# One operation of a search made one-input, and output weights split into their high and low parts once

## The chip, the cores and the metric

The kernel runs on one core of a Trainium2 chip. The metric is device time in microseconds (us), the median of several runs. TensorE (PE) multiplies matrices, PEld is its weight load; VectorE (DVE), ScalarE (ACT) and GpSimd (POOL) work on tiles; SyncE (SP) queues most transfers, POOL some of them.

## The reference

Three layers in a row, all float32: a linear attention with a norm, a mixture of eight experts in which every expert takes exactly 576 of 4608 tokens, and a layer that all tokens share.

```python
def _attn_ref(q, k, v, g_norm):
    kv = np.einsum('bhsd,bhse->bhde', k, v)
    out = np.einsum('bhsd,bhde->bhse', q, kv)
    rms = np.sqrt(np.mean(out * out, axis=-1, keepdims=True) + 1e-06)
    return (out / rms * g_norm).astype(np.float32)
...
def _moe_ref(x, w_gate, w1, w2):        # N=4608, D=512, E=8, F=1024
    cap = N // E
    logits = x @ w_gate
    order = np.argsort(-logits.flatten())
    # the highest logits first: a token goes to the expert of its highest logit that still has a place
    for e in range(E):
        out[assigned == e] = np.maximum(x[assigned == e] @ w1[e], 0.0) @ w2[e]
...
def _moe2_ref(x, w1, w2, w3, w_out):    # 512 -> 768 -> 512, weights shared by all tokens
    h = np.maximum(np.maximum(x @ w1, x @ w2), x @ w3)
    return (h @ w_out).astype(np.float32)
```

(The two lines on the assignment stand for a loop over the sorted logits.)

## The kernel before, in words

**Products.** Every large product is made of three matmuls on two float32r parts of each operand, `hi` (the value cast) and `lo` (value less `hi`): `mm3` (L823 to L825). One group is 12 such matmuls, [128x128] by [128x288].

**Stages.** Attention first; its rows go to the DRAM tile `xd`. Then one stage per expert, p = 0 to 7: gather the expert's 576 rows, w1 with relu (8 weight tiles), w2 (8 tiles), the shared layer's three products (18 tiles that stay in SBUF as `W3`), and the output product with the shared output weights `wo` (6 tiles). The tiles of w1, w2 and `wo` are streamed: `w_load` has SP fetch a [128x512] float32 tile into one of 3 buffers `raw`, and `w_split` makes `hi` (ACT, L349) and `lo` (POOL, L350, a subtraction with two inputs) in one of 6 buffers `ring`. So the six `wo` tiles are fetched and split again in each of the eight stages. `advance(n)` keeps splits three tiles ahead of PE.

**Routing beside it.** While stage p multiplies, the generator `phase(p + 1)` finds the next expert's tokens. `tick()` lets it go one piece further after each group of 12 matmuls, so its instructions stand between those of the stage in every engine's queue, in the order of the program. For p + 1 = 1 to 6 it runs `search` twice, with 11 and 5 steps. A step tests three thresholds: two counts on ACT (L490) and one on DVE (L492), `ce` (L496, DVE), a count over partitions on PE (L499), then on DVE `ex` (L503), `an` (L505), the step's sum `tot` (L507) and the next thresholds `T` (L511), for which L490 and L492 of the next step wait. A step spans two groups.

```python
nc.vector.scalar_tensor_tensor(ex[:, 0, 0:3], an, step, z, op0=OP.mult, op1=OP.add,
                               accum_out=tot)                      # L507, z is zeros
nc.vector.tensor_scalar(Tn, nx, T[:, 0:1], tot, op0=OP.add, op1=OP.add)   # L511
```

**The decoder.** The shared weights arrive as 64-bit words. `decoder` turns 24 tiles (18 of `W3`, 6 of `wo`, which stand first in `ORDER`, every second one) into float32 in the background, from the end of attention until the middle of stage 0: `dec_a` (ACT, L367 and L368, writes `dh` and `dr`), `dec_b` (DVE L376 and L378, POOL L379), `dec_c` one piece later, `dec_d` one more. A `W3` tile gets its `hi` in `dec_c` (ACT, L385) and its `lo` in `dec_d` (DVE, L393). A `wo` tile is stored in `dec_c` from POOL's queue into the DRAM tile `wod` (L387) and has nothing to do in `dec_d`.

Of the kernel before, what the change touches and what calls it, by code (L numbers as in the profile page):

```python
# [9 lines left out]
F32 = mybir.dt.float32  # L10
F32R = mybir.dt.float32r
# [4 lines left out]
OP = mybir.AluOpType  # L16
# [6 lines left out]
DM = NH * D  # L23
E = 8
FF = 1024
F2 = 768
# [10 lines left out]
def body(ctx: ExitStack, tc: tile.TileContext, qx, kx, vx, g, wg, w1, w2, w123, wo, out):  # L37
    nc = tc.nc
    consts = ctx.enter_context(tc.tile_pool(name="consts", bufs=1))
    dram = ctx.enter_context(tc.tile_pool(name="dram", bufs=1, space=DRAM))  # L40
    ctx.enter_context(tc.manual_schedule())

    xd = dram.tile([N, DM], F32, name="xd")
    wod = dram.tile([F2, DM], F32, name="wod")

    L = consts.tile([128, E, NT], F32, name="L")
    OWN = consts.tile([128, NT], F32, name="OWN")
# [18 lines left out]
    rt = ctx.enter_context(tc.tile_pool(name="rt", bufs=1))  # L66
# [93 lines left out]
    for s in range(2):  # L160
        p = slice(64 * s, 64 * s + 64)
        nc.vector.tensor_scalar(GW[p, :, s * E:s * E + E], wgt[p], gcol[p], None, op0=OP.mult)
    BD = []
    for i in range(2):
        t = ac.tile([128, NH // 2, 144], F32, name=f"BD{i}")
# [109 lines left out]
            nc.sync.dma_start(xd[c * 128:c * 128 + 128], xs)  # L275

    def keys(best, sh):
        """order-preserving integers of float32: the upper 32 - sh bits, the lower sh"""
        bi = best.bitcast(I32)
        sg, yy, hi, lo = (rt.tile([128, NT], I32, name="k" + str(i)) for i in range(4))  # L280
        sf = rt.tile([128, NT], F32, name="kf")
        nc.vector.tensor_scalar(sg, bi, 31, None, op0=OP.arith_shift_right)
        nc.vector.tensor_tensor(yy, bi, sg, op=OP.bitwise_xor)
        nc.vector.tensor_scalar(hi, yy, sh, None, op0=OP.arith_shift_right)
        nc.vector.tensor_scalar(lo, yy, 2 ** sh - 1, None, op0=OP.bitwise_and)
        nc.vector.tensor_scalar(sf, sg, 2.0 ** (31 - sh), 2.0 ** (31 - sh), op0=OP.mult, op1=OP.add)
        return sf, hi, lo

    def pick(V, oh, best, m):
        """one-hot of the first best expert"""  # L290
        def bb(ap):
            return ap[:, None, :].to_broadcast([128, E, NT])
        dv = desc[:, :, None].to_broadcast([128, E, NT])
        sc = rt.tile([128, E, NT], F32, name="scE")
        nc.vector.tensor_reduce(best, V.rearrange("p e c -> p c e"), axis=AX, op=OP.max)
        yield
        nc.vector.tensor_tensor(sc, V, bb(best), op=OP.is_equal)
        nc.vector.tensor_mul(sc, sc, dv)
        yield
        nc.vector.tensor_reduce(m, sc.rearrange("p e c -> p c e"), axis=AX, op=OP.max)  # L300
        nc.vector.tensor_tensor(oh, sc, bb(m), op=OP.is_equal)
        yield
# [45 lines left out]
    def split(raw, hi, lo, e):  # L348
        nc.scalar.copy(hi, raw)  # L349
        e.tensor_sub(lo, raw, hi)  # L350
# [3 lines left out]
    W3, XV = {}, {}  # L354
# [6 lines left out]
    def dec_a(i):  # L361
        while i not in W64:
            more64(1)
        w = W64.pop(i).rearrange("p (n t) -> p n t", t=2)
        h = early.tile([128, DM], F32, name="dh", bufs=3)
        r = early.tile([128, DM], I32, name="dr", bufs=5)
        nc.scalar.activation(h, w[:, :, 1].bitcast(F32), AF.Copy, scale=2.0 ** -112)  # L367
        nc.scalar.activation(r, w[:, :, 0].bitcast(U32), AF.Copy, scale=2.0 ** -29)  # L368
        XV[i] = (h.bitcast(I32), r)
        if i >= 18:  # L370
            late64.append(i - 6)
# [9 lines left out]
    def dec_c(i):  # L381
        v = XV[i][1].bitcast(F32)
        if i < 18:
            W3[i] = w3p.tile([128, 2, 512], F32R, name="w3_%d" % i, tag="w3_%d" % i)
            nc.scalar.copy(W3[i][:, 0], v)  # L385
        else:
            nc.gpsimd.dma_start(wod[(i - 18) * 128:(i - 17) * 128], v)  # L387

    def dec_d(i, e):
        v = XV.pop(i)[1].bitcast(F32)  # L390
        ready.append(i)
        if i < 18:
            e.tensor_sub(W3[i][:, 1], v, W3[i][:, 0])  # L393

    ORDER = [18, 0, 19, 1, 20, 2, 21, 3, 22, 4, 23, 5] + list(range(6, 18))
    ready, late64 = [], ORDER[12:18]
# [3 lines left out]
            load64(late64.pop(0))  # L400

    def decoder():
        """float64 words to float32, rounded to nearest, and to hi and lo"""
        for n in range(28):
            if n >= 4:
                dec_d(ORDER[n - 4], nc.vector)
            if 0 <= n - 3 < 24:
                dec_c(ORDER[n - 3])
            if n < 24:
                dec_a(ORDER[n])  # L410
            if 0 <= n - 2 < 24:
                yield from dec_b(ORDER[n - 2])
            yield
# [7 lines left out]
    for bp in range(NP):  # L421
# [31 lines left out]
        if bp == NP - 1:  # L453
# [3 lines left out]
            early = es.enter_context(tc.tile_pool(name="early", bufs=1, side="right"))  # L457
# [17 lines left out]
    ONE, IDX, IDXW = {}, {}, {}  # L475
# [2 lines left out]
        return ap[:, :, None].to_broadcast([128, E, NT])  # L478

    def search(KT, i0, i1, REM2):  # L480
        """the highest integer that leaves an expert with more keys from it on than it has places"""
        T = SC[:, i0]
        z = rt.tile([128, 3], F32, name="z")
        nc.vector.memset(z, 0.0)
        for i in range(i0, i1):
            cnt = rt.tile([96, 3], F32, name="cnt", bufs=2)
            gs = rt.tile([128, 36, 36], BF, name="W1", bufs=2)[0:96].rearrange("p a b -> p (a b)")
            gs = gs[:, 0:1152].rearrange("p (j a) -> p j a", j=3)
            for j in range(2):
                nc.scalar.activation(gs[:, j], KT, AF.Sign, bias=T[0:96, 1 + j:2 + j], scale=-1.0,  # L490
                                     accum_out=cnt[:, j:j + 1])
            nc.vector.tensor_scalar(gs[:, 2], KT, T[0:96, 3:4], -192.0, op0=OP.is_ge, op1=OP.add,  # L492
                                    accum_out=cnt[:, 2:3])
            yield
            ce = rt.tile([96, 3, E], BF, name="ce")
            nc.vector.tensor_mul(ce, BM, cnt[:, :, None].to_broadcast([96, 3, E]))  # L496
            yield
            pc = rps.tile([128, 512], F32, name="rps")
            nc.tensor.matmul(pc[:, :3 * E], ones[0:96], ce.rearrange("p j e -> p (j e)"), start=True, stop=True)  # L499
            ex = rt.tile([128, 3, E], F32, name="ex")  # L500
            an = rt.tile([128, 3], F32, name="an")
            tot = rt.tile([128, 1], F32, name="tot")
            nc.vector.tensor_tensor(ex, pc[:, :3 * E].rearrange("p (j e) -> p j e", e=E),  # L503
                                    REM2[:, None, :].to_broadcast([128, 3, E]), op=OP.is_gt)
            nc.vector.tensor_reduce(an, ex, axis=AX, op=OP.max)  # L505
            step = float(4 ** (10 - i) if i < 11 else 4 ** (15 - i))
            nc.vector.scalar_tensor_tensor(ex[:, 0, 0:3], an, step, z, op0=OP.mult, op1=OP.add,  # L507
                                           accum_out=tot)
            Tn = rt.tile([128, 4], F32, name="T4", bufs=2)
            nx = SC[:, i + 1] if i + 1 < i1 else SC[:, 16]  # L510
            nc.vector.tensor_scalar(Tn, nx, T[:, 0:1], tot, op0=OP.add, op1=OP.add)  # L511
            T = Tn
        yield T[:, 0:1]
# [7 lines left out]
        return dx  # L521

    def top_search(g2):
        """the first phase's search: thresholds at once, counted on the tensor engine"""
        def narrow(pc, J, i, K):
            ex = rt.tile([E, 64], BF, name="ex8")
            nc.vector.tensor_scalar(ex[:, 0:J], pc[0:E, 0:J], float(CAPN), None, op0=OP.is_gt)
# [12 lines left out]
        for it in range(6):  # L540
            if it == 4:
                K = rt.tile([128, NT], F32, name="K2")
                t = rt.tile([128, NT], F32, name="best")
# [200 lines left out]
    first = phase(0)  # L744
# [7 lines left out]
    stream = []  # L752
# [4 lines left out]
    RAW, RING, ROW = {}, {}, {}  # L757
    st = {"load": 0, "split": 0}

    def w_load():  # L760
        n = st["load"]
        st["load"] += 1
        p, kind, i = stream[n]
        raw = wr.tile([128, 512], F32, name="raw", bufs=3)
        RAW[n] = raw
        if kind == "wo":
            nc.sync.dma_start(raw, wod[i * 128:i * 128 + 128])
        else:
            if p not in ROW:
                ROW[p] = nc.values_load(IDXW[p][0:1, 0:1], engines=(mybir.EngineType.SP,), min_val=0,  # L770
                                        max_val=(E - 1) * 1024,
                                        skip_runtime_bounds_check_because="one of the experts")
            nc.sync.dma_start(raw, (w1 if kind == "w1" else w2)[bass.ds(ROW[p] + i * 128, 128), :])

    def w_split():
        n = st["split"]
        st["split"] += 1
        t = wr.tile([128, 2, 512], F32R, name="ring", bufs=6)
        split(RAW.pop(n), t[:, 0], t[:, 1], nc.gpsimd)
        RING[n] = t  # L780

    def advance(n):
# [36 lines left out]
        nc.vector.tensor_sub(X[:, :, 1, cs], src, X[:, :, 0, cs])  # L819

    def mm3(ps, wt, ws, x, xs, first, last):
        """exact products of hi and lo parts"""
        nc.tensor.matmul(ps, wt[:, 0, ws], x[:, 0, xs], start=first, stop=False)  # L823
        nc.tensor.matmul(ps, wt[:, 1, ws], x[:, 0, xs], start=False, stop=False)  # L824
        nc.tensor.matmul(ps, wt[:, 0, ws], x[:, 1, xs], start=False, stop=last)  # L825
# [198 lines left out]
```

## Time and profile before

| | before |
|---|---|
| median of 3 runs | 1310.72 us (1310.59 to 1311.41) |
| span of the profiled execution | 1307.6 us |
| what lies around the span (median less span) | 3.1 us |
| PE busy | 1200.0 us, 92% |
| DVE, ACT, POOL busy | 703.5, 503.3, 508.4 us |

No separate time is given for the profiled execution; its span is the first instruction to the last, and the median lies 3.1 us above it. Matmuls overlap in PE's pipeline, so PE's busy time says less than the distance from one matmul's start to the next.

### The profile page before, as it was taken

The page shows a single profiled execution, that of the slowest core. Times are in us where ns is not written, and L with a number is a line of the kernel's source. Part 1 is how long each engine was busy: PE and PEld are TensorE (multiplying, and loading weights), DVE is VectorE, ACT ScalarE, POOL GpSimd, SP SyncE. Part 2 cuts the span into 40 slices and gives each one's busy share as a digit, 9 for nine tenths or more (in the row PEclk, how much of TensorE's full clock was granted, in tenths as well). Part 3 has the DMA queues.
Part 4 walks back from the last instruction along what each step waited for, and adds up shares of the span by engine and source line. Part 5 has one row for each costly group of instructions (what it writes and reads, how often), then busy time and mean ns, then how long its engine had stood idle before and what let it go on. Part 6 is the DMA issues. An engine that isn't in the chain of part 4 may idle for free.

```text
span 1307.6 us, 23349 instructions
## 1 busy us (share of the span) xinstructions
PE 1200.0 (92%) x8814; PEld 1132.2 (87%) x8814; DVE 703.5 (54%) x2074; ACT 503.3 (38%) x1232; POOL 508.4 (39%) x539
## 2 busy tenths in 40 slices
PE   7796248899999999999999999999999999999997
PEld 6685238788889989998989998999899899989995
DVE  2799867897477427751776257734773231122110
ACT  3354426654354135522553245324541332133120
POOL 0456444434632435224422453145324372245231
PEclk9899559999999999999999999999999999999999
DMA  6978435400420113102320232013201151023101
GB/s 227 373 280 314 184 97 198 146 4 2 140 81 31 42 49 122 49 2 80 106 65 1 66 113 67 16 41 106 82 25 42 58 168 33 1 72 106 33 1 41
DMA packets 52689, 119.76 MB, mean 92 GB/s; under 512 B 6880, under 2 KB 11488, under 8 KB 51040
## 3 DMA queue, kind: packets, MB, share of 16 engines
q1 hardware_dynamic: 45712, 96.75, 22.4%
q0 software_dynamic: 6560, 21.50, 4.9%
q8 instruction: 69, 1.13, 0.4%
q14 instruction: 44, 0.36, 0.1%
q10 hardware_dynamic: 304, 0.02, 0.0%
HBM read 97.80 MB, written 20.45 MB: 90 GB/s over the span
## 4 chain that ended last, share of the span: by engine, by line
PE 60%; DVE 8%; ACT 4%; issue 3%; POOL 1%; DMA 0%; POOLq 0%; ACTq 0%; DVEq 0%
PE mm L823 16%; PE mm L825 16%; PE mm L824 16%; DVE ex L507 4%; ACT W L490 3%; PE mm L970 3%; PE mm L972 3%; PE mm L971 3%; PE tp L812 1%; DVE T L511 1%; DVE an L505 1%; DVE X L923 1%; DVE ex L503 0%; PE rps L615 0%; PE rps L499 0%
## 5 line engine op out<-in xcount | busy, mean ns | idle before, releaser
L823 PE MATMUL mm<-X,w 128*128 128x288 f32 x1152 | 345.3, 300 | 0.0
L350 POOL TENSOR_TENSOR ring<-raw,ring 128x512 fp32r<-128x512 f32 x176 | 228.8, 1305 | 299.6 <-ACT ring L349 285.9
L824 PE MATMUL mm<-X,w 128*128 128x288 f32 x1152 | 341.0, 296 | 1.5 <-DVE w L393 1.5
L825 PE MATMUL mm<-X,w 128*128 128x288 f32 x1152 | 341.1, 296 | 0.0
L824 PEld LDWEIGHTS mm<-X,w 128*128 128x128 f32 x1152 | 216.7, 188 | 2.2 <-DVE w L393 2.2
L823 PEld LDWEIGHTS mm<-X,w 128*128 128x128 f32 x1152 | 217.0, 188 | 0.4
L825 PEld LDWEIGHTS mm<-X,w 128*128 128x128 f32 x1152 | 216.4, 188 | 0.5
L947 POOL TENSOR_TENSOR H<-t,H 128x288 fp32r<-128x288 f32 x96 | 79.0, 823 | 339.3 <-ACT H L946 339.1
L945 DVE TENSOR_TENSOR t<-mm,t 128x288 f32<-128x288 f32 x192 | 87.0, 453 | 173.9 <-PE mm L825 173.6
L823 PE MATMUL mm<-X,ring 128*128 128x288 f32 x512 | 156.0, 305 | 2.1 <-ACT X L818 1.1
L823 PE MATMUL mm<-H,ring 128*128 128x288 f32 x512 | 155.5, 304 | 0.0
L824 PE MATMUL mm<-X,ring 128*128 128x288 f32 x512 | 152.2, 297 | 1.3 <-POOL ring L350 1.3
L825 PE MATMUL mm<-X,ring 128*128 128x288 f32 x512 | 152.4, 298 | 0.0
L824 PE MATMUL mm<-H,ring 128*128 128x288 f32 x512 | 151.3, 295 | 0.0
L825 PE MATMUL mm<-H,ring 128*128 128x288 f32 x512 | 151.2, 295 | 0.0
L490 ACT ACTIVATE W<-KT,T 96x384 bf16<-96x384 f32 x168 | 102.1, 608 | 126.2 <-DVE T L511 126.2
L946 ACT CAST H<-t 128x288 fp32r<-128x288 f32 x96 | 41.4, 431 | 255.0 <-DVE t L945 254.9
L349 ACT CAST ring<-raw 128x512 fp32r<-128x512 f32 x176 | 106.6, 615 | 6.3 <-DMA raw<-w_dram 6.3
L823 PEld LDWEIGHTS mm<-X,ring 128*128 128x128 f32 x512 | 97.9, 191 | 3.2 <-ACT X L818 1.9
L824 PEld LDWEIGHTS mm<-X,ring 128*128 128x128 f32 x512 | 97.6, 191 | 1.5 <-POOL ring L350 1.5
L825 PEld LDWEIGHTS mm<-X,ring 128*128 128x128 f32 x512 | 97.2, 190 | 0.3 <-DVE X L819 0.2
L823 PEld LDWEIGHTS mm<-H,ring 128*128 128x128 f32 x512 | 96.8, 189 | 0.0
(247 smaller groups left out, 2120.5 us busy)
## 6 DMA issues: line engine op xcount, KB each, us to landing
raw<-w_dram SPq DMA_DIRECT2D x128, 256.0 KB, 2.6
raw<-wod SPq DMA_DIRECT2D x48, 256.0 KB, 2.6
xd<-xs SPq DMA_DIRECT2D x36, 256.0 KB, 5.2
w<-w_dram SPq DMA_DIRECT2D x18, 512.0 KB, 4.7
qta<-qx_dram SPq DMA_DIRECT2D x4, 1280.0 KB, 11.1
qtb<-qx_dram SPq DMA_DIRECT2D x4, 1024.0 KB, 9.6
kta<-kx_dram SPq DMA_DIRECT2D x3, 1280.0 KB, 19.8
vta<-vx_dram SPq DMA_DIRECT2D x3, 1280.0 KB, 15.3
```

The lines of the kernel that those rows point to most:

```text
L349: nc.scalar.copy(hi, raw)
L350: e.tensor_sub(lo, raw, hi)
L490: nc.scalar.activation(gs[:, j], KT, AF.Sign, bias=T[0:96, 1 + j:2 + j], scale=-1.0, accum_out=cnt[:, j:j + 1])
L507: nc.vector.scalar_tensor_tensor(ex[:, 0, 0:3], an, step, z, op0=OP.mult, op1=OP.add, accum_out=tot)
L823: nc.tensor.matmul(ps, wt[:, 0, ws], x[:, 0, xs], start=first, stop=False)
L824: nc.tensor.matmul(ps, wt[:, 1, ws], x[:, 0, xs], start=False, stop=False)
L825: nc.tensor.matmul(ps, wt[:, 0, ws], x[:, 1, xs], start=False, stop=last)
L945: nc.vector.tensor_tensor(t2, ps[:, :HS], (t1, t1, t2)[j], op=OP.max)
L946: nc.scalar.copy(m[:, 0, cs], t2)
L947: nc.gpsimd.tensor_sub(m[:, 1, cs], t2, m[:, 0, cs])
L970: nc.tensor.matmul(pss[c], l[:, 0, ls], w[:, 0, :], start=(fc == 0), stop=False)
L971: nc.tensor.matmul(pss[c], l[:, 0, ls], w[:, 1, :], start=False, stop=False)
```

## The change

It does two things. The sum of a search step becomes a `tensor_scalar` that reads one tensor and also writes its sum; the tile of zeros `z` and its memset go. And the output weights are split once: `dec_c` casts a `wo` tile's `hi` into the old `dh` buffer (ACT), `dec_d` makes `lo` in `dr` (DVE) and stores both from POOL's queue into `wod`, which gets a middle dimension of 2; `dh` gets a fourth buffer. In the stages a `wo` tile is then fetched by one transfer of 512 KB straight into its `ring` buffer, in `w_split`, with no `raw` buffer and no split.

```diff
-    wod = dram.tile([F2, DM], F32, name="wod")
+    wod = dram.tile([F2, 2, DM], F32, name="wod")
...
-        h = early.tile([128, DM], F32, name="dh", bufs=3)
+        h = early.tile([128, DM], F32, name="dh", bufs=4)
...
         else:
-            nc.gpsimd.dma_start(wod[(i - 18) * 128:(i - 17) * 128], v)
+            nc.scalar.copy(XV[i][0].bitcast(F32R), v)
 
     def dec_d(i, e):
-        v = XV.pop(i)[1].bitcast(F32)
+        h, r = XV.pop(i)
+        v = r.bitcast(F32)
         ready.append(i)
         if i < 18:
             e.tensor_sub(W3[i][:, 1], v, W3[i][:, 0])
+        else:
+            e.tensor_sub(r.bitcast(F32R), v, h.bitcast(F32))
+            for j, t in enumerate((h, r)):
+                nc.gpsimd.dma_start(wod[(i - 18) * 128:(i - 17) * 128, j], t.bitcast(F32))
...
-        z = rt.tile([128, 3], F32, name="z")
-        nc.vector.memset(z, 0.0)
...
-            nc.vector.scalar_tensor_tensor(ex[:, 0, 0:3], an, step, z, op0=OP.mult, op1=OP.add,
-                                           accum_out=tot)
+            nc.vector.tensor_scalar(ex[:, 0, 0:3], an, step, 0.0, op0=OP.mult, op1=OP.add, accum_out=tot)
...
         p, kind, i = stream[n]
+        if kind == "wo":
+            return
         raw = wr.tile([128, 512], F32, name="raw", bufs=3)
         RAW[n] = raw
-        if kind == "wo":
-            nc.sync.dma_start(raw, wod[i * 128:i * 128 + 128])
...
         t = wr.tile([128, 2, 512], F32R, name="ring", bufs=6)
-        split(RAW.pop(n), t[:, 0], t[:, 1], nc.gpsimd)
+        if stream[n][1] == "wo":
+            i = stream[n][2]
+            nc.sync.dma_start(t.bitcast(F32), wod[i * 128:i * 128 + 128])
+        else:
+            split(RAW.pop(n), t[:, 0], t[:, 1], nc.gpsimd)
         RING[n] = t
```

On POOL, in stage 0 while the decoder runs (`dr` and `dh` are the decoder's buffers, L350 is the `lo` of a streamed tile), the order before is:

```order
L379 TENSOR_TENSOR dr<-dh,dr 128x512
L350 TENSOR_TENSOR ring<-raw,ring 128x512 x2
L379 TENSOR_TENSOR dr<-dh,dr 128x512
L350 TENSOR_TENSOR ring<-raw,ring 128x512
L387 DMA wod<-dr 128x512
L350 TENSOR_TENSOR ring<-raw,ring 128x512
L379 TENSOR_TENSOR dr<-dh,dr 128x512
```

and of the change, at the same place:

```order
L379 TENSOR_TENSOR dr<-dh,dr 128x512
L350 TENSOR_TENSOR ring<-raw,ring 128x512 x2
L379 TENSOR_TENSOR dr<-dh,dr 128x512
L350 TENSOR_TENSOR ring<-raw,ring 128x512
L398 DMA wod<-dh 128x512
L398 DMA wod<-dr 128x512
L350 TENSOR_TENSOR ring<-raw,ring 128x512
L379 TENSOR_TENSOR dr<-dh,dr 128x512
```

One store has become two, of the tile that was decoded one before, and the second waits for DVE's subtraction.

On ACT, in stage 0 (L902, L907 in the changed file, is the relu of a group; L490, L493 there, counts for the search), the order before is:

```order
L349 CAST ring<-raw 128x512
L902 ACTIVATE H<-mm 128x288
L367 ACTIVATE dh<-w_5_1386 128x512
L368 ACTIVATE dr<-w_5_1386 128x512
L902 ACTIVATE H<-mm 128x288
```

and of the change:

```order
L349 CAST ring<-raw 128x512
L907 ACTIVATE H<-mm 128x288
L387 CAST dh<-dr 128x512
L367 ACTIVATE dh<-w_5_1386 128x512
L368 ACTIVATE dr<-w_5_1386 128x512
L907 ACTIVATE H<-mm 128x288
```

A cast stands ahead of `dec_a`, whose two buffers are now those from which an earlier `wo` tile was stored.

On SP, at the end of stage 1's fetches (`idxw` holds the row of the next expert's weights, L773 fetches them), before:

```order
L773 DMA raw<-w_dram 128x512
L767 DMA raw<-wod 128x512 x6
L770 TENSOR_LOAD idxw
L773 ISA
L773 DMA raw<-w_dram 128x512
```

and of the change:

```order
L774 DMA raw<-w_dram 128x512
L782 DMA ring<-wod 128x1024 x4
L771 TENSOR_LOAD idxw
L774 ISA
L774 DMA raw<-w_dram 128x512
L782 DMA ring<-wod 128x1024
L774 ISA
L774 DMA raw<-w_dram 128x512
L782 DMA ring<-wod 128x1024
```

Two of the six `wo` fetches now stand behind the next expert's first fetches, and all six go to `ring`.

## Rows read from the trace of the kernel before

**Rows 1.** The page: span, and busy time of PE and its weight load.

```profile
span 1307.6 us, 23349 instructions
...
PE 1200.0 (92%) x8814; PEld 1132.2 (87%) x8814; DVE 703.5 (54%) x2074; ACT 503.3 (38%) x1232; POOL 508.4 (39%) x539
```

**Rows 2.** Windows: stretch, length, busy us (instructions) by engine, granted clock, DMA share, GB/s.

```profile
370.00:402.00 32.00, 29.36 (x213) 27.52 (x213) 24.44 (x78) 17.54 (x50) 11.56 (x9) 1.00 0.22 67
```

**Rows 3.** Waits of PEld, from 370 to 402, 205 to 300, whole run: us, times, longest.

```profile
PEld L499 <- DVE ce L496: 4.5, 8, 0.7
...
PEld L499 <- DVE ce L496: 11.7, 11, 1.9
...
PEld L499 <- DVE ce L496: 35.4, 56, 1.9
```

**Rows 4.** Timeline of PE around two steps: start, us, instruction, idle before it.

```profile
373.00 0.29 PE L825 MATMUL mm<-H,ring 128*128 128x288 f32 x1
373.74 0.19 PE L499 MATMUL rps<-ce,ones 96*128 96x24 bf16 x1 [0.44 <-DVE ce L496]
...
388.39 0.29 PE L825 MATMUL mm<-H,ring 128*128 128x288 f32 x1
388.82 0.19 PE L499 MATMUL rps<-ce,ones 96*128 96x24 bf16 x1
```

**Rows 5.** Timeline of POOL, DVE and ACT, one search step from 370 to 375.

```profile
370.43 1.28 POOL L350 TENSOR_TENSOR ring<-raw,ring 128x512 fp32r<-128x512 f32 x1 [2.64 <-ACT ring L349]
370.67 1.06 DVE L507 SCALAR_TENSOR_TENSOR ex<-an,z 128x3 f32<-128x3 f32 x1
371.77 0.29 DVE L511 TENSOR_SCALAR T<-SC,T,tot 128x4 f32<-128x4 f32 x1
372.16 0.62 ACT L490 ACTIVATE W<-KT,T 96x384 bf16<-96x384 f32 x1 [1.50 <-DVE T L511]
373.66 0.61 ACT L349 CAST ring<-raw 128x512 fp32r<-128x512 f32 x1
374.35 1.29 POOL L350 TENSOR_TENSOR ring<-raw,ring 128x512 fp32r<-128x512 f32 x1 [2.63 <-ACT ring L349]
```

**Rows 6.** Timeline of DVE, a step of the second search.

```profile
407.59 0.16 DVE L507 SCALAR_TENSOR_TENSOR ex<-an,z 128x3 f32<-128x3 f32 x1
...
407.79 0.29 DVE L511 TENSOR_SCALAR T<-SC,tot 128x4 f32<-128x4 f32 x1
```

**Rows 7.** Timeline of POOL and DVE in stage 0, from 229 to 231.

```profile
229.07 1.29 POOL L350 TENSOR_TENSOR ring<-raw,ring 128x512 fp32r<-128x512 f32 x1 [2.64 <-ACT ring L349]
229.41 0.97 DVE L507 SCALAR_TENSOR_TENSOR ex<-an,z 128x3 f32<-128x3 f32 x1
230.32 1.28 POOL L379 TENSOR_TENSOR dr<-dh,dr 128x512 int32<-128x512 int32 x1
230.43 1.20 DVE L511 TENSOR_SCALAR T<-SC,T,tot 128x4 f32<-128x4 f32 x1
```

**Rows 8.** Timeline of POOL and DVE in stage 0, at 256.

```profile
256.34 1.28 POOL L379 TENSOR_TENSOR dr<-dh,dr 128x512 int32<-128x512 int32 x1
256.44 0.61 DVE L492 TENSOR_SCALAR_CACHE_REDUCE W<-KT,T 96x384 bf16<-96x384 f32 x1
```

**Rows 9.** Timeline of PE and DVE in the first expert's top search.

```profile
154.06 0.17 PE L530 MATMUL rps<-ex,ones 8*128 8x15 bf16 x1 [0.25 <-DVE ex L527]
...
157.69 0.68 DVE L393 TENSOR_TENSOR w<-dr,w 128x512 fp32r<-128x512 f32 x1
...
158.83 0.17 PE L530 MATMUL rps<-ex,ones 8*128 8x15 bf16 x1 [0.56 <-DVE ex L527]
```

**Rows 10.** The stores of L387 by their landing; POOL and ACT where two of them fall.

```profile
DMA to landing us min/median/max: 2.5/3.9/4.5
...
225.12 1.30 POOL L350 TENSOR_TENSOR ring<-raw,ring 128x512 fp32r<-128x512 f32 x1 [2.03 <-ACT ring L349]
...
233.74 0.68 ACT L367 ACTIVATE dh<-w 128x512 f32<-128x512 f32 x1
```

**Rows 11.** The page's DMA issues: count, KB each, median us to landing.

```profile
w<-w_dram SPq DMA_DIRECT2D x18, 512.0 KB, 4.7
```

More of the change, by code (lines that the diff above doesn't have):

```diff
@@ L763, in w_load @@
         p, kind, i = stream[n]
+        if kind == "wo":
+            return
         raw = wr.tile([128, 512], F32, name="raw", bufs=3)
         RAW[n] = raw
-        if kind == "wo":
-            nc.sync.dma_start(raw, wod[i * 128:i * 128 + 128])
[L768 to L773, printed above, removed]
+        if p not in ROW:
+            ROW[p] = nc.values_load(IDXW[p][0:1, 0:1], engines=(mybir.EngineType.SP,), min_val=0,
+                                    max_val=(E - 1) * 1024,
+                                    skip_runtime_bounds_check_because="one of the experts")
+        nc.sync.dma_start(raw, (w1 if kind == "w1" else w2)[bass.ds(ROW[p] + i * 128, 128), :])
     def w_split():
```

## The prediction

> **What bounds the kernel now.** I read the page first: PE is busy for 1200.0 of 1307.6 us, the next engine for 703.5 [rows 1]. So the time can only move where PE stands still, or where its work changes; the change leaves PE's work alone. The windows come next. From about 300 us on PE stands still in one kind of stretch only, the second half of stages 1 to 5, where the search runs beside the products: from 370 to 402 it is busy for 29.36 of 32.00 us at full granted clock [rows 2]. The waits of its weight load say for what: `ce` of the count at L499, 4.5 us in 8 waits there, 11.7 us in 11 in stage 0, 35.4 in the whole run [rows 3]. Five stages and stage 0 make 34.2 of these 35.4. Of a wait's length a little is hidden in the pipeline, so I count PE's loss from starts: one matmul follows another by 0.13 us, L499 starts 0.74 after the last one, so 0.61 is lost; two steps later in the pattern 0.30 [rows 4]. The eight gaps of that stage are 0.61, 0.60, 0.32, 0.59, 0.30, 0.61, 0.30, 0.61, together 3.9 us; five such stages hold 19.5, and stage 0 another 11.
>
> What makes `ce` late is one step's timeline. L507 needs 0.16 us [rows 6], but takes 1.06 when POOL subtracts at the same time: it started at 370.67, POOL's L350 had started at 370.43 and ended at 371.71, and L507 ended at 371.73 [rows 5]. A DVE operation with two inputs in SBUF is held until POOL's operation ends. Then come the read of the sum and L511, 0.29, so that `T` is there 0.35 after POOL, and ACT's next count (L490) starts at 372.16 [rows 5]. ACT waits for `T`, `ce` for ACT, PE for `ce`, and the next split is queued behind PE's next group: a loop whose longest link at each held step is POOL's subtraction.
>
> **The sum of a step.** L507 gets one tensor instead of two. Its work should stay at 0.16; the nearest row is L492, also a `tensor_scalar` that writes its sum, on 128 times as many elements a lane: 0.61 [rows 8]. That is a ceiling of 0.61 and a floor of nothing saved; I take 0.16, since three elements cost what the old form on three costs. Whether it is held is told by the same row: POOL's L379 ran from 256.34 to 257.62, L492 started at 256.44 and took its usual 0.61 [rows 8]. So the new L507 is not held, and is done with its read about 0.26 after it starts.
>
> But right behind it stands L511, a plain `tensor_scalar`, and stage 0 shows that this one is held too: it took 1.20 instead of 0.29 and ended at 231.63, when POOL's L379, begun at 230.32, ended at 231.60 [rows 7]. So the wait doesn't go away, it moves one instruction down. L511 will stand there while POOL subtracts and end 0.04 after it, instead of 0.35: what is saved at a held step is 0.31, the read and L511's own work, which now lie under POOL's. Two bounds: L511 not held at all (the whole gap goes), or the new L507 held after all (nothing).
>
> 0.31 off each gap of the stage makes 0.30, 0.29, 0.01, 0.28, 0, 0.30 for the first six, 1.18 together. The last two follow steps in which the splits are those of `wo`; these splits go (next part), so nothing is held there and both gaps close. The stage loses 3.92 less 1.18, that is 2.74; five stages 13.7 us.
>
> **Weights split once.** Per `wo` tile and stage this removes a cast on ACT, 0.61, and a subtraction on POOL, 1.29 [rows 5]: 48 of each, 29 us of ACT and 62 of POOL. By itself that is worth nothing, since PE is ahead of neither; what counts is three subtractions per stage that fall into the search, already counted in the two closed gaps. The price is a fetch of 512 KB instead of 256 KB. The nearest row of that size lands in 4.7 us [rows 11], at a DMA share of 0.22 in such a stretch [rows 2]. A `wo` tile's `ring` buffer is free from the products of w2 on, tens of us before PE comes to the output product, so a fetch of 4.7, or of twice that, is hidden by the 18 tiles of `W3` that PE works on between. On SP two of the six fetches now stand behind the next expert's row number and first w1 fetches; these wait for nothing that they did not wait for before, and the `wo` tile behind them is needed a whole product later. I cost this at nothing; without that cover each late tile would cost PE its landing.
>
> **The decoder.** Each of six `wo` tiles gains a cast on ACT (0.61, by L349), a subtraction on DVE (0.68, by L393) and a second store; 12 memsets of `z` go, on an idle DVE. In the top search of the first expert a DVE subtraction of this kind, L393, lengthened PE's wait from 0.25 to 0.56 [rows 9]; two of the new ones fall there: 0.7. Three of the casts fall in stage 0's search, where ACT's counts are in the chain: up to 0.61 each, I take 0.5, so 1.5. The other subtractions meet a DVE that waits for ACT: 0 to 1.2, I take 0.5. Together 2.7, from 0.7 to 4.
>
> Stage 0 also gains. In five steps there POOL runs L350 and L379, or two L350, back to back; today L507 is held by the first and L511 by the second, as at 229.41 and 230.43 [rows 7]. Now L511 alone has to get in, and it can after the first: L507 ended at 230.38 although L379 had begun at 230.32 [rows 7], so an operation that already waits goes ahead of the next one on POOL. That is 1.2 a step, as far as the gap behind it reaches: the gaps are 0.74, 1.31, 1.13, 1.30 and 1.80, so 0.74 + 1.2 + 1.13 + 1.2 + 1.2, about 5.5. Bounds: 0, if the second on POOL gets in first, and 11, all of stage 0's gaps. The Trainium skill, "SBUF — State Buffer", section "Who interferes with whom", says that DVE and GpSimd share one pair of ports as an exclusive lock, and that whoever issues first keeps it for the whole instruction. By issue order alone the waiting L511 has it before L379, which is what the row shows; by a reading in which POOL's queue holds on to it, 5.5 would be 0.
>
> **Sum.** 13.7 + 5.5 - 2.7 = 16.5 us less. The profiled span of 1307.6 becomes 1291.1, and with the 3.1 us by which the median lies above that span [rows 1], 1294.2.
>
> **The rivals.**
>
> *L511 escapes as well.* If it is held only where it is the second of two, all 19.5 us in five stages go, 6 or more in stage 0, less 2.7: 23 us, 1287.8. Against it: the L511 of rows 7 started while L379 was 0.11 us old and was held to its end; the new one meets L350 in the same way.
>
> *The new sum is held too*, so the change doesn't do what it says. Then only the two gaps behind the `wo` splits close, 0.91 in each of five stages, 4.5, less 2.7: about 1309, not to be told from before. Against it speaks L492 of rows 8, which differs in its shape and in an output of half the width.
>
> *Slower: ACT waits for the stores.* `dec_a` writes the buffers from which a `wo` tile was stored, one step earlier than before. The second of the two stores stands in POOL's queue behind an L350 such as that at 225.12 (done at 226.42) and DVE's subtraction; with up to 1.6 us for the latter it goes at 226.5 to 228. The stores of today land in 3.9, at most 4.5 [rows 10]: by 232.5 at the latest. The L367 that needs the buffer starts at 233.74 [rows 10], so the slack is 1.2 us or more. If stores land later than that, ACT stands at L367, behind it the relu that frees PSUM and the counts of the search, and PE waits. Three tiles are exposed. To eat 16.5 us each would have to be held for 5.5, that is landing after 239.2, some 11 us after issue, over twice the longest of today. At 14 us each tile waits 8.3, and the time is about 1319. The Trainium skill, "SBUF — State Buffer", box "The 'DVE blocks DMA' trap (SWDGE)", says that a store queued by GpSimd can't have its descriptors written while DVE holds the shared ports; by its two figures (620 ns alone, 3100 overlapped) an estimate is 2.5 us more a store, a wait of up to 1.3 us a tile, and 1298 in place of 1294. None of the six stores of today is that late [rows 10].
>
> *Half the gain.* The loop of a stage could settle on another pace: with the counts sooner, ACT's casts and counts meet in another order, and 0.15 instead of 0.31 is saved a step, or stage 0 gains nothing. That is 8 to 11 us: 1300 to 1303.
>
> **How the numbers follow.** A measurement of this kernel can tell about 0.2%, 2.6 us. Chances: L511 takes over the wait 0.62, L511 escapes 0.12, half the gain 0.13, sum still held 0.08, stores late 0.05. The time of the likeliest is 1294.2, its own range 1290 to 1299 (its bounds of 4 and 0.7 for the decoder, of 0 and 8 for stage 0). From 1287 to 1303 leaves out the two on the slow side, 0.13, and a little beyond escape. Faster 0.87, same 0.08, slower 0.05.
>
> **What the profile after would show.** L507 at 0.16 to 0.2 in nearly all its 96 instances, and L511 at up to 1.1 in held steps, ending when POOL's L350 ends. PEld's wait at L499 down from 35.4 to some 12 to 15. L349 and L350 at 128 instances instead of 176. In a stage of 1 to 5, eight gaps with 1.2 us in all. Two waits at L530 longer by 0.3. It would be wrong if L511 stays at 0.29 beside POOL (faster than I say), if L507 still reaches 1.06 (no change), if ACT's L367 waits for a DMA from `dh` or `dr`, or if PE waits for `ring` from a DMA in the output product.

## The result, and the profile after

The changed kernel takes 1288.87 us, median of 4 runs (1288.18 to 1290.69), against 1311.07 us for the kernel before beside it. The ratio is 0.9827, interval 0.9810 to 0.9844: 22.2 us less, where 16.5 less were forecast. The time lies in the stated range, near its lower end, and below the 1290 to 1299 given for the likeliest case.

The page of the profile after answers to [rows 1]: PE's work is the same, POOL and ACT have less.

```profile
span 1288.9 us, 23207 instructions
...
PE 1197.7 (93%) x8814; PEld 1134.3 (88%) x8814; DVE 675.3 (52%) x2068; ACT 481.8 (37%) x1190; POOL 450.3 (35%) x497
```

Next the waits of PEld after (us in total, times, longest). In the changed file `ce` is L499 and its count L502.

```profile
PEld L502 <- DVE ce L499: 11.9, 24, 1.3
```

35.4 us in 56 waits [rows 3] have become 11.9 in 24. Where they went is told by the two lines of the change, by form (ns min/median/max): L510 is the sum, L513 the next thresholds `T` (L507 and L511 before).

```profile
L510 DVE TENSOR_SCALAR_CACHE_REDUCE ex<-an x96: 155/156/158, 222.8 to 956.5; 128x3 f32<-128x3 f32 x96
...
L513 DVE TENSOR_SCALAR T<-SC,T,tot x84: 287/428/1353, 226.6 to 956.7; 128x4 f32<-128x4 f32 x84
...
L513 DVE TENSOR_SCALAR T<-SC,tot x12: 287/290/827, 223.0 to 943.5; 128x4 f32<-128x4 f32 x12
```

The sum is never held: 158 ns at most in 96 steps, where L507 took 1.06 us [rows 5]. `T` is held in its place. One step, from the timelines of POOL and DVE (start, us):

```profile
373.56 1.29 POOL L350 TENSOR_TENSOR ring<-raw,ring 128x512 fp32r<-128x512 f32 x1 [2.31 <-ACT ring L349]
...
373.80 0.16 DVE L510 TENSOR_SCALAR_CACHE_REDUCE ex<-an 128x3 f32<-128x3 f32 x1
373.88 0.08 DVE L510 DVE_READ_ACCUMULATOR ex<-an 128x1 f32 x1
374.00 0.87 DVE L513 TENSOR_SCALAR T<-SC,T,tot 128x4 f32<-128x4 f32 x1
```

POOL's subtraction ends at 374.85, L513 at 374.87: 0.02 behind it. Before, `T` stood 0.35 behind POOL [rows 5]. PE's side of two steps in that stage:

```profile
376.55 0.19 PE L502 MATMUL rps<-ce,ones 96*128 96x24 bf16 x1
379.87 0.19 PE L502 MATMUL rps<-ce,ones 96*128 96x24 bf16 x1
383.43 0.19 PE L502 MATMUL rps<-ce,ones 96*128 96x24 bf16 x1
```

The steps are 3.32 and 3.56 us apart; 3.32 is the step in which PE waits for nothing. Of nine gaps, 4.1 us with the first of 0.18, three are left: 0.28, 0.24 and 0.25.

**Where the time went.** Whole profiled spans hold a difference that isn't the change's: the first count of the top search, ahead of which the change touches almost nothing, starts at 143.00 after, at 139.55 before. It starts at 143.00 in the kernel with the sum alone too, which changes nothing ahead of it. So I measure from there, by the starts of PE: first count of the top search, first and 16th count of the search in stage 0, 96th count (stage 5), last matmul. For the changed kernel:

```profile
143.00 0.21 PE L532 MATMUL rps<-ex,ones 8*128 8x63 bf16 x1 [0.30 <-DVE ex L529]
...
222.13 0.19 PE L502 MATMUL rps<-ce,ones 96*128 96x24 bf16 x1
...
281.12 0.19 PE L502 MATMUL rps<-ce,ones 96*128 96x24 bf16 x1
...
955.83 0.19 PE L502 MATMUL rps<-ce,ones 96*128 96x24 bf16 x1
...
1278.59 0.40 PE L977 MATMUL mm<-ring,H 128*128 128x512 f32 x1
```

The distances of such rows, in us, for each kernel (the experiments are told below):

| | to the search | stage 0's search | to the 96th count | to the end | sum |
|---|---|---|---|---|---|
| before | 77.91 | 63.95 | 692.64 | 323.66 | 1158.16 |
| after | 79.13 | 58.99 | 674.71 | 322.76 | 1135.59 |
| sum alone | 77.84 | 61.59 | 676.83 | 323.66 | 1139.92 |
| wo alone | 80.71 | 63.28 | 688.38 | 323.67 | 1156.04 |
| places alone | 77.94 | 63.82 | 691.37 | 322.76 | 1155.89 |
| after, old places | 80.81 | 59.04 | 676.11 | 323.66 | 1139.62 |
| decoder's work alone | 79.49 | 64.15 | 693.15 | 323.66 | 1160.45 |
| after, `T` freed | 79.19 | 58.73 | 670.44 | 322.76 | 1131.12 |
| after, `T` and `ce` freed | 79.36 | 60.27 | 670.48 | 322.75 | 1132.86 |

After less before: +1.22, -4.96, -17.93 and -0.90, together -22.57, which agrees with the 22.2 of the medians. The -0.90, in the column "to the end", was a surprise: no search runs there, and nothing was forecast.

### The profile page after: what moved, and what is told of

It reads as the page before. It is cut to its first block, busy times and chain, and to the rows that moved or that the text cites. A ratio compares the mean times of both kernels' runs of the same rounds, so it can differ in the third digit from the quotient of the medians.

```text
span 1288.9 us, 23207 instructions
## 1 busy us (share of the span) xinstructions
PE 1197.7 (93%) x8814; PEld 1134.3 (88%) x8814; DVE 675.3 (52%) x2068; ACT 481.8 (37%) x1190; POOL 450.3 (35%) x497
## 4 chain that ended last, share of the span: by engine, by line
PE 64%; DVE 5%; ACT 3%; issue 3%; POOL 1%; POOLq 0%; ACTq 0%; DVEq 0%
PE mm L828 18%; PE mm L829 17%; PE mm L830 17%; PE mm L975 3%; PE mm L977 3%; PE mm L976 3%; ACT W L493 3%; DVE T L513 2%; PE tp L817 1%; DVE an L508 1%; DVE ex L510 0%; PE rps L617 0%; DVE ex L506 0%; DVE X L928 0%; DVE H L910 0%
## 5 line engine op out<-in xcount | busy, mean ns | idle before, releaser
L350 POOL TENSOR_TENSOR ring<-raw,ring 128x512 fp32r<-128x512 f32 x128 | 167.5, 1311 | 259.3 <-ACT ring L349 237.3
L493 ACT ACTIVATE W<-KT,T 96x384 bf16<-96x384 f32 x168 | 102.1, 609 | 107.0 <-DVE T L513 107.0
L828 PEld LDWEIGHTS mm<-H,ring 128*128 128x128 f32 x512 | 96.8, 189 | 0.0
L829 PEld LDWEIGHTS mm<-H,ring 128*128 128x128 f32 x512 | 96.4, 188 | 0.0
```

## The experiments

**What bounds each half of the change.** The main theory: the two-input sum was the held operation, and `T` now takes its place. The rival: the three splits that left each search freed it. The first two kernels make one half each.

The sum alone, with `z` kept so that no tile moves:

```diff
-            nc.vector.scalar_tensor_tensor(ex[:, 0, 0:3], an, step, z, op0=OP.mult, op1=OP.add,
-                                           accum_out=tot)
+            nc.vector.tensor_scalar(ex[:, 0, 0:3], an, step, 0.0, op0=OP.mult, op1=OP.add, accum_out=tot)
```

> The kernel before with the one-input step sum alone; z and its memset stay, so that no tile moves, and the wo tiles are split in every stage as before. By the theory of the prediction (the wait moves from the sum to the T operation, 0.3 us shorter a step, and in stage 0 one hold takes the place of two) it carries most of the gain: some 3.0 us in each of five stages and 5 in stage 0, 18 to 21 us less, 1290 to 1293. By the rival that it is the removal of the wo splits that frees the search, it gains under 8 us, above 1303. In the trace: the sum at 0.16 us in all 96 instances, the T operation at up to 1.2.

Measured: 1294.54 us against 1312.86, ratio 0.9861 (0.9843 to 0.9880), 18.3 us less. This half carries most of the gain, so the rival falls. Its waits of PEld, and its `T` operation by form (L510 in this file):

```profile
PEld L499 <- DVE ce L496: 15.7, 29, 2.3
```

```profile
L510 DVE TENSOR_SCALAR T<-SC,T,tot x84: 288/765/1326, 225.2 to 960.1; 128x4 f32<-128x4 f32 x84
```

Here the median step is a held one, 765 ns. By stretch (table): 2.4 us off in stage 0, where 5 were expected, and 15.8 in the five stages, where 15 were. In stage 0 the wait moved one operation further in two steps: `ce`, which has two inputs as well and takes 0.18 us alone, was held by POOL for 1.28 and 1.25, and PE's gaps there are 1.68 and 2.25 us. The second stands beside the split of a `wo` tile:

```profile
258.45 1.46 POOL L350 TENSOR_TENSOR ring<-raw,ring 128x512 fp32r<-128x512 f32 x1
...
258.69 1.25 DVE L496 TENSOR_TENSOR ce<-BM,cnt 96x24 bf16<-96x24 f32 x1
```

The output weights alone, the old sum and `z` put back into the changed kernel (the diff above, reversed):

> The changed kernel with the old two-input step sum and z put back: the output weights alone are split once. By the theory the two gaps behind the old wo splits close, 0.9 us in each of five stages, 4.5 in all, and the decoder costs 1 to 2.7: 1.8 to 3.5 us less, 1307.5 to 1309.5. By the rival that fewer splits free the search as a whole it gains 10 us or more. If the stores held up the decoder, it would be slower than before.

Measured: 1310.20 us against 1312.86, ratio 0.9976 (0.9965 to 0.9987), 2.7 us less by the medians and 3.2 by the ratio, as the theory had it. The old sum is held as ever where POOL still splits:

```profile
L512 DVE SCALAR_TENSOR_TENSOR ex<-an,z x96: 161/268/1082, 221.8 to 973.5; 128x3 f32<-128x3 f32 x96
```

The median fell from 0.9 us to 0.27, because the steps behind the `wo` splits are free; the longest is the same 1.08. The table has 4.3 us off in the five stages and 0.7 in stage 0, and 2.8 added ahead of the search.

**The gain where no search runs.** In the changed kernel the matmuls of the shared products follow one another faster. Two theories: less work on the other engines, or the place of the tiles, since without `z` all that is allocated behind it (X, H, `raw`, `ring`) lies 32 bytes lower. Two kernels, one that moves only the tiles, and one that changes everything but their place:

```diff
-    SC = consts.tile([128, 17, 4], F32, name="SC")
+    SC = consts.tile([128, 18, 4], F32, name="SC")
...
-        z = rt.tile([128, 3], F32, name="z")
-        nc.vector.memset(z, 0.0)
+        z = SC[:, 17, 0:3]
```

The second is the changed kernel with the two removed lines put back; nothing reads its `z`.

> The kernel before in which z is a row of the constant tile SC instead of a tile of its own: no instruction of the steps changes (only 12 memsets go), but X, H, raw and ring lie 32 bytes lower, as in the changed kernel. The trace after shows the matmuls of the shared products 0.8 ns closer to each other than before, in stages 6 and 7 as well, where no search runs: some 0.33 us in each of eight stages. If the place of the tiles makes this, 2.0 to 3.0 us less, 1308 to 1309; if the missing splits or the smaller load on the other engines do, no change, 1311.

> The changed kernel with the tile z and its memset kept, unused: X, H, raw and ring lie where they lay before. If their place makes the shared products faster, 2.0 to 3.0 us more than the changed kernel, 1291 to 1292; if not, the same as it, 1288.9.

Measured: the move alone 1309.58 us against 1312.86, ratio 0.9981 (0.9969 to 0.9992), 3.3 us less by the medians and 2.5 by the ratio; the changed kernel with the old places 1293.37, ratio 0.9857 (0.9839 to 0.9876), 19.5 less than before instead of 22.2 by the medians. First and last matmul of the last stage's shared product, 432 in all, with the tiles moved:

```profile
1218.95 0.29 PE L822 MATMUL mm<-X,w 128*128 128x288 f32 x1
...
1276.05 0.29 PE L824 MATMUL mm<-X,w 128*128 128x288 f32 x1
```

and in the changed kernel with the old places:

```profile
1202.07 0.30 PE L830 MATMUL mm<-X,w 128*128 128x288 f32 x1
...
1259.54 0.30 PE L832 MATMUL mm<-X,w 128*128 128x288 f32 x1
```

57.10 us against 57.47: 0.37 us a stage. The pitch (the distance from one matmul's start to the next) is 132.5 ns with the tiles moved and 133.3 without, in stages 6 and 7 of all kernels of either kind, whichever work the other engines had. So the place of the tiles makes it. Why is open: two more places were looked at, with an unused tile ahead of X in the kernel of the next experiment.

> The kernel with the freed T operation and an unused tile of 64 bytes ahead of X, H, raw and ring: X starts at 68512, 32 above the place before and 64 above that of the changed kernel. If the pitch of the shared products goes by the place modulo 64 bytes, it is 132.5 ns as in the changed kernel; if lower is better, 133.3 or more.

> The same with 96 bytes: X at 68544. If the pitch goes by the place modulo 64, 133.3 ns as in the kernel before; otherwise 132.5 or another figure.

The pitches were 132.8 and 132.6 ns (single times 1288.4 and 1283.6 us). By the place modulo 64 bytes they should have been 132.5 and 133.3: that rule falls. So does the rule that lower is better, since 132.6 at the highest place is less than 132.8 and 133.3 below it. I have no other.

**Is it the hold of `T` that is left?** `T` can take the form that isn't held, if the sum starts from T's first column:

```diff
-            nc.vector.tensor_scalar(ex[:, 0, 0:3], an, step, 0.0, op0=OP.mult, op1=OP.add, accum_out=tot)
+            nc.vector.tensor_scalar(ex[:, 0, 0:3], an, step, T[:, 0:1], op0=OP.mult, op1=OP.add, accum_out=tot)
...
-            nc.vector.tensor_scalar(Tn, nx, T[:, 0:1], tot, op0=OP.add, op1=OP.add)
+            nc.vector.tensor_scalar(Tn, nx, tot, 0.0, op0=OP.add, op1=OP.add, accum_out=an[:, 0:1])
```

> The changed kernel in which the T operation is freed as well: the sum starts from T's first column and so gives T + sum, and the T operation adds that to its constants and writes a sum of its own that nobody reads, the form that was not held in the count beside POOL. Same results, same places of the tiles. If the hold by POOL is what is left of the wait, the gaps of 0.28, 0.24 and 0.25 us go, 0.8 in each of five stages, 4 in all, and 1 to 3 of stage 0's 6: 3.5 to 7 us less than the changed kernel, 1282 to 1285.5 where before is 1311. If the T operation is held in any form, or the gaps come from the counts on ACT, no change: 1289. In the trace the T operation would stand at about 0.3 us in all 96 instances.

Measured: 1285.12 us against 1312.84, ratio 0.9783 (0.9760 to 0.9805); its interval lies below that of the changed kernel. `T` by form, and the waits of PEld:

```profile
L513 DVE TENSOR_SCALAR_CACHE_REDUCE T<-SC,tot x96: 216/217/220, 223.0 to 952.2; 128x4 f32<-128x4 f32 x96
```

```profile
PEld L502 <- DVE ce L499: 6.6, 11, 1.2
```

The longest `T` fell from 1353 to 220 ns, in the same steps beside the same POOL work. In stages 1 to 5 no gap above 0.02 us is left at the counts, 4.3 us less (table), where 4 were expected. All 6.6 us that remain are in stage 0, which gained 0.3 where 1 to 3 were expected. There the next operation with two inputs is seen held:

```profile
254.34 1.27 POOL L379 TENSOR_TENSOR dr<-dh,dr 128x512 int32<-128x512 int32 x1 [3.23 <-DVE dh L378]
...
254.41 1.23 DVE L499 TENSOR_TENSOR ce<-BM,cnt 96x24 bf16<-96x24 f32 x1 [0.16 <-ACT W L493]
```

`ce` is held in six steps of stage 0 here, not in three as the next expectation has it: 1.23 to 1.27 us in five, 0.78 in one. Before and after the change it is held in two (1.20 and 0.78 in each). So `ce` was freed as well, on top of this:

```diff
-            cnt = rt.tile([96, 3], F32, name="cnt", bufs=2)
+            cnt = rt.tile([96, 4], F32, name="cnt", bufs=2)
...
-            nc.vector.tensor_mul(ce, BM, cnt[:, :, None].to_broadcast([96, 3, E]))
+            for j in (2, 0, 1):
+                nc.vector.tensor_scalar(ce[:, j], BM[:, j], cnt[:, j:j + 1], 0.0, op0=OP.mult, op1=OP.add,
+                                        accum_out=cnt[:, 3:4])
```

> The kernel with the freed T operation, in which the next two-input operation of the step is freed too: ce is made by three one-input operations that also write a sum (one per threshold, the one whose count ends last at the end) instead of one product of two tiles. In the profile with the freed T operation, ce took 1.23 instead of 0.18 us in three steps of stage 0 beside POOL's decoder. If that hold is what is left in stage 0, 1 to 3 us less than with the freed T operation alone, that is 26 to 29 us... worked out against before: 1282 to 1285 where before is 1312.8. If three operations in place of one lengthen the chain, 0 to 3 us more than with the freed T operation, and PE's gaps come back in stages 1 to 5.

Measured: 1287.50 us against 1312.64, ratio 0.9815 (0.9802 to 0.9829). That is 2.4 us slower than with `T` freed alone by the medians, with intervals that just overlap, and 1.7 in the profiles (table). The three operations of one step:

```profile
246.00 0.21 DVE L500 TENSOR_SCALAR_CACHE_REDUCE ce<-BM,cnt 96x8 bf16<-96x8 f32 x1
...
246.34 0.22 DVE L500 TENSOR_SCALAR_CACHE_REDUCE ce<-BM,cnt 96x8 bf16<-96x8 f32 x1
...
246.68 0.22 DVE L500 TENSOR_SCALAR_CACHE_REDUCE ce<-BM,cnt 96x8 bf16<-96x8 f32 x1
```

They stand 0.34 apart, so `ce` is done 0.7 later in every step, and that costs stage 0 more than its six holds did: 60.27 us instead of 58.73. PE's gaps did not come back in stages 1 to 5 (one of 0.09 in 80 steps), so these have nearly that much slack.

**The price of the decoder.** The kernel before with the new casts and subtractions, whose results are dropped, and the fourth `dh` buffer (the `wo` tile is stored and split as before):

```diff
...
+            nc.scalar.copy(XV[i][0].bitcast(F32R), v)
             nc.gpsimd.dma_start(wod[(i - 18) * 128:(i - 17) * 128], v)
...
+            e.tensor_sub(h.bitcast(F32R), v, h.bitcast(F32))
```

> The kernel before with the decoder's new work alone: the six casts on ACT and six subtractions on DVE are made and their results dropped, the wo tile is stored once and split in each stage as before. It prices the term of 2.7 us (0.7 to 4) of the prediction: 0.7 to 4 us more than the kernel before, 1311.8 to 1315. If that work is hidden, no change, and then the later start of the first search seen in the profiles with the wo change is another thing (the second store, the clock).

Measured: 1314.76 us against 1312.84, ratio 1.0014 (1.0002 to 1.0027), 1.9 us more. The profile has 1.6 more ahead of the search, 0.2 in stage 0's search and 0.5 in the five stages.

## Why the prediction was right, and where its sizes were off

**The wait moves to `T`: right, and shown.** The sum is free in all 96 steps, `T` ends 0.02 behind POOL, and when `T` takes the form with a sum of its own the remaining wait in stages 1 to 5 goes. That also settles the two rivals beside it: against "the new sum is held too", no sum took above 158 ns; against "`T` escapes", which had `T` held only behind two operations of POOL in a row, the `T` at 374.00 took 0.87 behind a single one. The measured 22.2 us is close to the 23 of that second rival by chance, and is not made by it; from the time alone one would have picked the wrong one. The Trainium skill, "SBUF — State Buffer", section "Who interferes with whom", lists `tensor_scalar` among the operations that can take the shared ports, and excepts the form that also writes out its accumulator; 1353 against 220 ns agrees.

**The term of 13.7 us for five stages was too small:** 17.9. About 3.3 us a stage is the search, where 2.74 was put, the rest the place of the tiles. (The eight gaps as I listed them add up to 3.94, not 3.92, which makes 2.76 a stage and 13.8.) The step that failed is "0.31 off each gap": I left out the gap of 0.18 at the first held step, and let each step keep its own 0.31. What a step gains beyond its own gap makes the next start sooner. The rows of one step show it; POOL's operation of before is the one at 370.43 in [rows 5]. First PE's count before, then the count and POOL after:

```profile
369.82 0.19 PE L499 MATMUL rps<-ce,ones 96*128 96x24 bf16 x1
```

```profile
369.61 0.19 PE L502 MATMUL rps<-ce,ones 96*128 96x24 bf16 x1
...
369.97 1.29 POOL L350 TENSOR_TENSOR ring<-raw,ring 128x512 fp32r<-128x512 f32 x1 [2.31 <-ACT ring L349]
```

POOL's subtraction starts 0.36 us behind the count, where it was 0.61: 0.25 sooner, and `T` is there 0.33 sooner behind POOL. So the next gap closed wholly (0.61 to 0.01, where 0.30 was left to it), and from there the stage alternates between 0 and a quarter.

**The place of the tiles was missing.** "12 memsets of `z`, on an idle DVE" was right for the instructions, but the tile's 32 bytes moved X: 2.3 us by the stretches of the move alone (0.1 in stage 0, 1.3 and 0.9), 2.5 to 3.3 in its times. It is over a third of the 5.7 us by which I was off.

**The split of `wo` was added as a term of its own, where it overlaps with the sum.** With the old sum its removal gives the 0.9 a stage that I put (4.3 in five). With the new sum the same steps had little left to lose: the sum alone leaves gaps of 1.1 us a stage, both together 0.8.

**Stage 0: 5.5 us were put to the sum, which alone gained 2.4;** with the `wo` change it is 5.0. One way in which that change helps is in the rows: it removes the split that held `ce` in the kernel with the sum alone (258.45 there), and PE's gap at that step goes from 2.25 to 0.01. That 5.0 lies near 5.5 is luck. The five gaps that I counted gave 3.1 of it, and the first of them grew, from 0.74 to 1.28, as it does to 1.22 with the decoder's work alone. Most of the rest came from gaps between them, which I had left as they were.

The idea that a waiting `T` gets in ahead of POOL's next operation holds in three steps of stage 0, as here (POOL's L350 began at 233.89, its L379 at 235.13):

```profile
234.37 0.82 DVE L513 TENSOR_SCALAR T<-SC,T,tot 128x4 f32<-128x4 f32 x1
```

and fails in one, at 226.55, where L379 began at 226.59 and `T` was held to its end:

```profile
226.55 1.35 DVE L513 TENSOR_SCALAR T<-SC,T,tot 128x4 f32<-128x4 f32 x1
```

The first had waited 0.76 when L379 began, the second 0.04. By the issue order that I went by, the second should have been first as well. With the sum alone, waits of 0.21 to 0.72 got in and one of 0.02 did not; where between 0.04 and 0.21 the line lies, and why, is open.

**The decoder's cost** of 2.7 (0.7 to 4) measured 1.9. Two of PE's waits at the top search did grow to 0.56, as forecast. The parts came out otherwise: of the 1.5 for casts in stage 0's search 0.2 is seen, and ahead of the search 1.6 where 0.7 was named. The profiles with the `wo` change differ there: 1.1 to 1.5 us in five, 2.8 and 2.9 in two (wo alone; after, old places). In those two the granted clock was 0.50, the level of 1.2 GHz, from 210 to 215 us, against 0.69 in the changed kernel, a part at each level; PE had been busy for 1.4 and 1.8 of the 5 us before, and for 2.6 in the changed kernel. Whether the clock makes the difference was not tried.

**The stores** were no danger: no wait of ACT's L367 for a DMA in the trace. They landed in 2.4 to 5.3 us, median 3.8, where it was 2.5 to 4.5 and 3.9 [rows 10]. So the estimate of 2.5 us more a store, and with it the 1298, did not come true. Its two figures stand in the Trainium skill, "SBUF — State Buffer", in the section "A bandwidth-pool intuition that's wrong (but worth ruling out)", not in the box. The fetches of 512 KB landed in 3.1 to 7.0 us, and PE never waited for a `wo` tile in `ring`: nothing, as put.

## What to carry to other kernels

When an operation is held by another engine, look at what stands behind it in the chain: the wait moves there, unless that one is of a free form too. Here it moved from the sum to `T`, and in stage 0 on to `ce`. What is gained then is the work between the two, in every step, and a step passes on what its own gap does not need: with the sum alone, 0.33 us a step closed about three quarters of the gaps in stages 1 to 5. Removing a tile moves all that is allocated behind it; to price an edit alone, keep its tile, and measure the shift by itself. And a total near one theory's number is no evidence for it: the durations of the two lines told the theories apart, the time did not.

## What was not expected of the hardware

The pitch of the same matmuls, at a granted clock of 1.00 (the level of 2.4 GHz), changes with where X lies, the tile that they stream past the weights: 132.5, 133.3, 132.8 and 132.6 ns with X at 68448, 68480, 68512 and 68544 bytes of its partition. The last two were seen in one profile each. The shared weights stayed where they were; `raw`, `ring`, H and the small tiles of the search moved along with X, so X was not moved by itself, and why the pitch changes is open. In 3456 matmuls the first two differ by 2.8 us.
